# Attention's steps queued per engine, and one weight tile converted per unit instead of two

## The chip, the cores and the metric

One core of a Trainium2 chip. The metric is the device time of one execution in microseconds (us); the kernel before takes 925.54 us, the median of 3 runs (923.69 to 925.55).

Engines are named as in the profile: PE is TensorE's matmul and PEld its weight load, DVE is VectorE, ACT is ScalarE, POOL is GpSimd, SP is SyncE, which issues most transfers.

## The reference

Windowed attention, then two expert layers without routing, one after the other:

```python
# attention: B 4, H 8, S 576, D 64; window 128, one slope per head
scores = where(mask, q @ k.T / sqrt(D) + bias, -1e9)
attn = softmax(scores)                       # over the keys
x = (attn @ v).transpose(0, 2, 1, 3).reshape(2304, 512)
# first layer, d_ff 2048
h = x @ w_in
g = (a0 + a1*h + a2*h*h + a3*h*h*h) / (1 + |b0|*|h| + |b1|*h*h + 1e-6)
x = g @ w_out
# second layer: the same shapes, with elu(h) in place of g
```

The weights of both layers are 64-bit floats in memory, so each tile of them is converted on the chip.

## The kernel before

**Attention.** 16 units of work, each one batch and one pair of heads (`units`). The steps of a unit have short names:
- `qT`, `kT`, `zT`: PE transposes of q, of k and of their last 64 rows (L438, L452); `qC`, `kC`, `zC`: copies of these from PSUM (ACT, DVE, DVE).
- `S0` to `S4`: the scores (PE, L494, L476); `D0` to `D8`: bias and row maximum (DVE, L520, one input in PSUM); `E0` to `E8`: the exponential with its sum (ACT, L535); `R0`, `R1`: the inverse sums (DVE); `N0` to `N8`: the normalising (POOL, L552).
- `T00` to `T11`: 16 transposes of the probabilities (PE, L568); `C00` to `C11`: their copies from PSUM (ACT, L461); `V0`, `V1`, `Y`: the products with v (PE, L587, L598); `XC`, `XY`: their copies into `xT` (ACT, DVE).

`STEPS` is one list for all engines: in each turn `t` of the loop every step is issued once, for unit `t + late`. Each engine keeps that order in its own queue.

**Conversion.** One of the first layer's 32 weight tiles (16 of `w_in`, "wi", and 16 of `w_out`, "wo") takes five operations on 128x512 words: `s` scale (ACT, L130), `a` shift (DVE, L138), `b` or (DVE, L148), `h` the rounded high part (DVE, L156, or ACT, L158), `l` the low part, high part subtracted (DVE, L162). `PLAN` puts two tiles into each of turns 5 to 14. Six further steps of `conv_step` (`CONV_AFTER`) follow in the last turns, and the rest in the first layer, one `conv_step` at every second chunk (`f % 2`). A tile passes `conv_step` in three calls: scale, then shift and or with the next call, high and low part after that.

**First layer.** 5 blocks of tokens (`BL`; block 0 is the first 512 tokens, from batch 0 alone), each with 16 chunks of d_ff. For a chunk `s`, `gemm1(s)` is 12 matmuls into a PSUM bank (`w_in`: high and low parts of weight and token, three products), `rational(s)` is the polynomial quotient, spread over ACT and DVE with the last operation `low` of the chunk before (L339) on POOL from `c > 4` on, and `gemm2_T(s - 3)` is 12 matmuls into the accumulators. The first four chunks of `gemm1` are computed at the end of the attention (`early`, `AHEAD`), and so are `rational(0)` and the first half of `rational(1)` (`FIRST`). Blocks 1 and 2 convert the second layer's weights beside the quotient (`joins`, `load_half`).

**Second layer.** A block scheme with fewer products (`second`), planned by costs written in the code; the change doesn't touch it.

The tiles of weights as loaded (512 KB each) come by SP's queue, two a turn from turn 2 to 13; so do q, k and v (per unit two transfers of 128 KB and one of 32 KB for the last rows of each).

Of the kernel before, what the change touches and what calls it, by code (L numbers as in the profile page):

```python
# [17 lines left out]
STEPS = (  # L18
# [10 lines left out]
)  # L29


PLAN = (0,) * 5 + (2,) * 10 + (0,) * 4
CONV_AFTER = ((15, "E8"), (15, "R1"), (14, "V1"), (15, "T01"), (15, "T11"), (15, "V1"))
AHEAD = {
    (14, "T00"): 1, (14, "T10"): 1, (14, "T11"): 2, (14, "V0"): 1, (14, "V1"): 2, (14, "Y"): 1,
}
ENG = {
    "h0": "D", "h1": "D", "l0": "D", "l1": "D", "qC": "A", "kC": "D",
    "zC": "D", "XC": "A", "XY": "D", "C00": "A", "C01": "A", "C10": "A", "C11": "A",
}  # L40
FIRST = {"r0": (14, "Y"), "r1": (15, "C11")}


@with_exitstack
def kernel(
# [13 lines left out]
    nc = tc.nc  # L59
# [34 lines left out]
    order = [(w, f) for f in range(KF) for w in ("wi", "wo")]  # L94
# [80 lines left out]
    def conv_step(keys, more=True, later=False, eng="A"):  # L175
# [128 lines left out]
    def rational(c, old=True, beside=4 * (lambda: None,)):  # L304
# [38 lines left out]


    def attention():
        with ExitStack() as es:
# [4 lines left out]
            vt = [raw.tile([P, NF + 1, 2, D], F32, name=f"v{n}") for n in range(2)]  # L351
            for t in vt:
                nc.gpsimd.memset(t[TL:P, NF], 0.0)
            units = [(b, p) for p in range(NP) for b in range(B)]
# [4 lines left out]
            qk_tails = place(LATE[3], [P, 3, 2, 2, D], F32, "qk_tails")  # L359

            def load(u, what):
# [3 lines left out]
                for nm in what:  # L365

                    eng = nc.scalar if u < 2 and nm == "k" else nc.sync
                    src = {"q": q, "k": k, "v": v}[nm]
                    if nm == "v":
                        t = raw_t[nm, u] = vt[u % 2]  # L370
                        body, tail = t[:, 0:NF], t[0:TL, NF]
                    else:
                        n = "qk".index(nm)
                        body, tail = raw_t[nm, u] = rows_qk[:, n], qk_tails[0:TL, u % 3, n]
                    for e in range(2):
# [4 lines left out]
                    eng.dma_start(  # L380
                        out=tail,
                        in_=src[b, 2 * p:2 * p + 2, NF * P:S, :].rearrange("h p d -> p h d"),
                    )


# [63 lines left out]
            def qk_tail_T(u):  # L449
                for n, nm in enumerate("qk"):  # L450
                    _, r = raw_t.pop((nm, u))
                    nc.tensor.transpose(  # L452
                        ty[:, n, :], r.rearrange("p e d -> p (e d)"), ident[0:TL, 0:TL]
                    )

            def qk_tail_copy(u):
                copy(ENG["zC"], qkT_t[u][:, :, NF * P:S], ty[:, 0:2, :])
# [119 lines left out]
            def attn_v(i0):  # L577
                def run(u):
                    vr = raw_t["v", u]
                    if i0 == 0:  # L580
# [13 lines left out]
            def attn_v_tail(u):  # L594
                vr = raw_t.pop(("v", u))
                for j in (NF - 1, NF):
                    for e in range(2):
                        nc.tensor.matmul(  # L598
                            ty[e * D:(e + 1) * D, 2, :], lhsT=vr[:, j, e, :],
# [4 lines left out]
            def x_copy(u):  # L604
                b, p = units[u]
                copy("D" if u > NU - 4 else ENG["XC"], xT[:, p, b * S:b * S + NF * P], x_t.pop(u).rearrange("p i c -> p (i c)"))

            def x_tail_copy(eng):
# [733 lines left out]
```

## Time and profile before

| stretch of the span, us | what runs | PE busy | DVE busy | ACT busy | POOL busy |
|---|---|---|---|---|---|
| 0 to 157.0 | attention, 26 tiles scaled, early chunks | 93% | 88% | 90% | 54% |
| 157.0 to 245 | first layer, block 0 | 100% | 93% | 84% | 23% |
| 245 to 400 | first layer, blocks 1 and 2 | 100% | 94% | 84% | 27% |
| 400 to 922.4 | the rest of it, second layer | 99% | 80% | 70% | 7% |

The profiled execution took 924.2 us; its span, from the first to the last instruction, is 922.4 us, and 1.8 us lie around it. TensorE's granted clock is 1.000, the 2.4 GHz level, all the way. A busy share is an average; what limits a stretch is read from the waits in it and from what follows at once on what.

### The profile page before, as it was taken

To read this page: it belongs to the slowest core of one execution; us is meant where nothing else is said; L and a number is where in the kernel's file an instruction comes from. 1 tells how busy PE (TensorE), PEld (TensorE's weight loads), DVE (VectorE), ACT (ScalarE), POOL (GpSimd) and SP (SyncE) were. 2 spreads that over 40 slices of the span, in tenths; PEclk is the share of its full clock that TensorE was granted. 3 is DMA by queue.
4 is the path that set the end of the run, shared out by engine and by line. 5 is a ranking of instruction groups with operands and counts; after the bars stand their busy time and mean duration, and the time that the engine had idled before them with its cause. 6 is when DMAs were issued, how large, how long until landed. Compare 5 with 4: busy or idle time off the path is not lost.

```text
span 922.4 us, 15561 instructions
## 1 busy us (share of the span) xinstructions
PE 907.6 (98%) x5110; PEld 772.2 (84%) x5110; DVE 786.0 (85%) x1761; ACT 710.3 (77%) x1514; POOL 184.5 (20%) x246
## 2 busy tenths in 40 slices
PE   8999998999999999999999999999999999999998
PEld 5777766888888888889988888989888898988887
DVE  7699999999899989978998979999877788677653
ACT  6999997888888888879887877667786667767553
POOL 4566661123222322232322210000000000000000
PEclk9999999999999999999999999999999999999999
DMA  8899971001344244400000124445253323342201
GB/s 157 207 244 217 258 218 53 1 1 34 103 138 138 72 134 130 144 25 1 7 29 0 58 92 128 147 149 194 80 181 101 118 81 111 130 149 84 78 0 69
DMA packets 112561, 98.28 MB, mean 107 GB/s; under 512 B 62816, under 2 KB 86368, under 8 KB 112480
## 3 DMA queue, kind: packets, MB, share of 16 engines
q1 hardware_dynamic: 109936, 96.57, 36.0%
q10 hardware_dynamic: 2544, 0.72, 0.4%
q8 instruction: 40, 0.66, 0.3%
q14 instruction: 41, 0.34, 0.1%
HBM read 79.96 MB, written 17.30 MB: 105 GB/s over the span
## 4 chain that ended last, share of the span: by engine, by line
PE 84%; DVE 11%; ACT 3%; issue 1%; DMA 0%; POOL 0%; ACTq 0%; DVEq 0%; POOLq 0%
PE acc L956 21%; PE acc L730 21%; PE h L289 20%; PE m L940 19%; DVE cvt L148 1%; DVE pr_wi L520 1%; DVE pr_wo L520 1%; PE s_ps L494 1%; PE ps_pT L568 1%; DVE w_wi L162 1%; ACT pr_wo L535 1%; PE x L587 1%; ACT pT L461 1%; DMA qk_tails_wo<-in_k_dram 0%; PE ps_qk L438 0%
## 5 line engine op out<-in xcount | busy, mean ns | idle before, releaser
L730 PE MATMUL acc<-space_g,w_wo 128*128 128x512 f32 (+1 forms) x960 | 210.7, 368 | 2.7 <-DVE space_g L339 2.3
L730 PEld LDWEIGHTS acc<-space_g,w_wo 128*128 128x128 f32 x960 | 168.2, 189 | 33.3 <-DVE space_g L339 2.8
L339 POOL TENSOR_TENSOR space_g<-xT,space_r 128x512 fp32r<-128x512 f32 (+1 forms) x76 | 89.7, 1180 | 295.1 <-DVE xT L338 200.1
L956 PE MATMUL acc<-op_wo,space_g 128*128 128x512 f32 x432 | 108.2, 393 | 0.0
L956 PEld LDWEIGHTS acc<-op_wo,space_g 128*128 128x128 f32 x432 | 80.4, 188 | 14.7
L289 PE MATMUL h<-space_qa,w_wi 128*128 128x512 f32 (+1 forms) x320 | 91.7, 370 | 0.4 <-DVE space_qa L266 0.4
L1002 ACT ACTIVATE space_u<-space_r 128x384 f32<-128x384 f32 x48 | 25.1, 522 | 75.3 <-DVE space_r L996 74.4
L313 ACT ACTIVATE space_u<-h 128x512 f32<-128x512 f32 (+1 forms) x80 | 44.3, 554 | 46.9 <-PE h L289 29.0
L940 PE MATMUL m<-xo_wi,op_wi 128*128 128x384 f32 x336 | 77.3, 337 | 0.0
L940 PE MATMUL m<-xo_wo,op_wi 128*128 128x384 f32 x336 | 76.4, 335 | 0.0
L289 PE MATMUL h<-space_qb,w_wi 128*128 128x512 f32 (+1 forms) x240 | 75.5, 369 | 0.1
L289 PE MATMUL h<-space_ta,w_wi 128*128 128x512 f32 (+1 forms) x240 | 75.4, 368 | 0.0
L325 DVE SCALAR_TENSOR_TENSOR xT<-space_u,b_abs,qa 128x512 f32<-128x512 f32 (+1 forms) x76 | 52.2, 687 | 20.1 <-ACT qa L314 19.9
L289 PEld LDWEIGHTS h<-space_qa,w_wi 128*128 128x128 f32 x320 | 57.7, 189 | 10.8 <-DVE space_qa L266 0.6
L940 PEld LDWEIGHTS m<-xo_wo,op_wi 128*128 128x128 f32 x336 | 60.9, 188 | 4.1
L940 PEld LDWEIGHTS m<-xo_wi,op_wi 128*128 128x128 f32 x336 | 60.5, 188 | 0.0
L322 DVE TENSOR_TENSOR space_g<-xT,space_r 128x512 fp32r<-128x512 f32 (+1 forms) x80 | 55.0, 687 | 5.3
L328 ACT ACTIVATE space_r<-xT,c_q 128x512 f32<-128x512 f32 (+1 forms) x80 | 55.3, 691 | 5.5 <-DVE xT L325 5.3
L315 ACT ACTIVATE xT<-h,a_sb 128x512 f32<-128x512 f32 (+1 forms) x80 | 59.2, 740 | 0.0
L289 PE MATMUL h<-space_bi,w_wi 128*128 128x512 f32 (+1 forms) x160 | 59.0, 369 | 0.2 <-POOL space_bi L269 0.2
L1006 ACT ACTIVATE space_u<-space_u,c_m 128x384 f32<-128x384 f32 x96 | 57.5, 611 | 1.6
L316 ACT ACTIVATE h<-h,a_sb 128x512 f32<-128x512 f32 (+1 forms) x80 | 57.3, 716 | 0.0
(189 smaller groups left out, 2121.8 us busy)
## 6 DMA issues: line engine op xcount, KB each, us to landing
space_qa<-joined_wo SPq DMA_DIRECT2D x43, 256.0 KB, 2.7
raw_wo<-in_moe_w_out_dram SPq DMA_DIRECT2D x20, 512.0 KB, 5.1
raw_wi<-in_moe_w_in_dram SPq DMA_DIRECT2D x16, 512.0 KB, 4.6
half<-in_moe_w_in_dram SPq DMA_DIRECT2D x32, 256.0 KB, 2.8
two_wo<-joined_wi SPq DMA_DIRECT2D x32, 256.0 KB, 2.9
s<-sums SPq DMA_DIRECT2D x32, 256.0 KB, 2.8
half<-in_moe_w_out_dram SPq DMA_DIRECT2D x22, 256.0 KB, 2.9
v<-in_v_dram SPq DMA_DIRECT2D x32, 128.0 KB, 3.6
```

Of the source, the lines that this page charges most:

```text
L289: nc.tensor.matmul(h, lhsT=WT["wi", f][:, SEL[wp], kk * P:(kk + 1) * P], rhs=x[xp][kk], start=(kk == 0 and n == 0), stop=(kk == KD - 1 and ...
L313: nc.scalar.activation(out=h2, in_=h, func=AF.Square)
L315: nc.scalar.activation(out=ee, in_=h, func=AF.Identity, scale=a_sb[:, 1:2], bias=a_sb[:, 0:1])
L316: nc.scalar.activation(out=h, in_=h, func=AF.Identity, scale=a_sb[:, 3:4], bias=a_sb[:, 2:3])
L322: nc.vector.tensor_tensor(out=hi, in0=ee0, in1=rr0, op=ALU.mult)
L325: nc.vector.scalar_tensor_tensor(out=qq, in0=h2, scalar=b_abs[:, 1:2], in1=qa, op0=ALU.mult, op1=ALU.add)
L328: nc.scalar.activation(out=rr, in_=qq, func=AF.Ln, bias=c_q)
L339: (nc.gpsimd if c > 4 else nc.vector).tensor_tensor(out=low, in0=ee0, in1=rr0, op=ALU.mult)
L730: nc.tensor.matmul(acc_t[d], lhsT=WT["wo", f][:, SEL[wp], d * P:(d + 1) * P], rhs=gt[SEL[xp]], start=(f == 0 and n == 0), stop=(f == KF - ...
L940: nc.tensor.matmul(out, lhsT=w[:, SEL[wp], c0:c0 + P], rhs=XO[q // NP2, nm, k][:, SEL[xp]], start=(k == 0 and n == 0), stop=(k == 1 and n ...
L956: nc.tensor.matmul(acc_t[T, t], lhsT=gt[SEL[xp]][:, t * P:(t + 1) * P], rhs=w[:, SEL[wp]], start=(first and n == 0), stop=(last and n == 2),)
L1006: nc.scalar.activation(out=e, in_=e, func=AF.Identity, bias=c_m)
```

## The change

- **Order.** `STEPS`, `PLAN`, `CONV_AFTER`, `AHEAD` and `FIRST` go. `QUEUES` has one list per engine with the lateness of each step, `NEEDS` what must have been issued before a step; the loop at the end of `attention` issues from the four lists whatever is ready, so each engine has its own order.
- **Units** run batch by batch: the four head pairs of batch 0 first. Block 0 needs no later batch. The 16 quarters of the early `gemm1` (`g0` to `g15`), the split of block 0's tokens (`xh`, `xA`, `xl`), the quotient of chunks 0 and 1 (`r0`, `r1`) and the second half of chunk 0's (`o0` to `o3`) become steps of the lists.
- **Conversion.** One tile each for units 1 to 15 (`s0`, `a0`, `b0`, `h0`, `l0`), its low part on POOL (`l0`); the other 17 in block 0: two calls of `conv_step` in chunks 2 to 5, one in chunks 6 to 16, their low part on POOL as well, and ahead of shift and or. `order` puts `wo` three places back.
- **Copies.** 22 of the 64 copies of transposed probabilities and 4 of the 16 of `XC` go to DVE (`ON_DVE`; before, 3 of `XC`). `R0` and `R1` become one `R`.
- **`rational`** gives `low` to POOL from `c > 2` on.
- **Loads.** The last rows of q, k and v come for two units at a time; one weight tile per unit is loaded from unit 0 on, four after unit 14's products with v, the last 13 after unit 15's. The second layer's first halves are loaded at chunk 16 (before, 14), and `joins` skips chunks 17 and 40 in place of 24 and 40.

```diff
+QUEUES = {
+    "PE": (
+        ("g8", 1), ("g2", 2), ("g14", -3), ("g15", -3), ("S4", 3), ("g3", 2), ("g11", -1), ("g12", -2),
+        ("g9", 1), ("Y", 1), ("V1", 1), ("V0", 1), ("kT", 4), ("g4", 2), ("g13", -2), ("T01", 2),
+        ("g5", 2), ("zT", 4), ("T00", 2), ("g0", 3), ("S0", 4), ("S1", 4), ("qT", 5), ("g6", 2),
+        ("T10", 2), ("g1", 3), ("g7", 2), ("T11", 2), ("S2", 4), ("S3", 4), ("g10", 1),
+    ),
+    "ACT": (
+        ("qC", 5), ("XC", 1), ("r0a", 3), ("E3", 4), ("E2", 4), ("E4", 4), ("E8", 4), ("E6", 4),
+        ("E5", 4), ("r1a", 2), ("r1c", -3), ("E7", 4), ("C01", 3), ("xA3", 4), ("xA1", 5), ("C00", 3),
+        ("E0", 4), ("r0c", 3), ("s0", 4), ("E1", 5), ("C10", 3), ("C11", 3),
+    ),
+    "DVE": (
+        ("r1d", -3), ("xh0", 4), ("xl0", 3), ("r0b", 2), ("D5", 3), ("D7", 3), ("b0", 2), ("kC", 4),
+        ("zC", 4), ("D0", 3), ("F01", 2), ("XY", 1), ("o3", -3), ("F00", 2), ("xl1", 3), ("xh2", 3),
+        ("o2", -1), ("r1b", -2), ("D1", 4), ("D3", 4), ("xl2", 3), ("o1", 0), ("R", 3), ("D2", 4),
+        ("o0", 1), ("D4", 4), ("F10", 2), ("xl3", 3), ("r0d", 2), ("F11", 2), ("h0", 2), ("a0", 3),
+        ("D8", 4), ("XD", 1), ("D6", 4),
+    ),
+    "POOL": (
+        ("N0", 2), ("N5", 2), ("N7", 2), ("N1", 2), ("N3", 2), ("N2", 2), ("N6", 2), ("N4", 2),
+        ("N8", 2), ("l0", 1),
+    ),
 }
...
-    order = [(w, f) for f in range(KF) for w in ("wi", "wo")]
+    order = sorted([(w, f) for f in range(KF) for w in ("wi", "wo")], key=lambda k: k[1] + 3 * (k[0] == "wo"))
...
+        if whole:
+            put_off.append(lambda: conv_lo(whole))
         if scaled:
             put_off.append(lambda: conv_shift(scaled))
             put_off.append(lambda: conv_or(scaled))
-        if whole:
-            put_off.append(lambda: conv_lo(whole, "D"))
...
-            (nc.gpsimd if c > 4 else nc.vector).tensor_tensor(out=low, in0=ee0, in1=rr0, op=ALU.mult)
+            (nc.gpsimd if c > 2 else nc.vector).tensor_tensor(out=low, in0=ee0, in1=rr0, op=ALU.mult)
...
-            units = [(b, p) for p in range(NP) for b in range(B)]
+            units = [(b, p) for b in range(B) for p in range(NP)]
...
+            def loads(step, u):
+                if step in ("qT", "kT", "zT") and {(n, u) for n in ("qT", "kT", "zT")} <= gone:
+                    if u + 3 < NU:
+                        load(u + 3, "qk")
+                    if u < NU - 1:
+                        load_some(1)
...
+                elif step in ("V0", "V1", "Y") and {(n, u) for n in ("V0", "V1", "Y")} <= gone:
+                    if u + 2 < NU:
+                        load(u + 2, "v")
+                    else:
+                        load_some(4 if u < NU - 1 else len(to_load))
...
+            while any(queues.values()):
+                for engine, queue in queues.items():
+                    if queue and ready(*queue[0]):
+                        step, u = queue.pop(0)
+                        gone.add((step, u))
...
-            if s >= NCH or f in (0, 8, KF - 1) or s < KF or width(s) < WB or s >= LAST + 3:
+            if s >= NCH or f in (0, KF - 1) or s in (KF + 1, 2 * KF + 8) or s < KF or width(s) < WB or s >= LAST + 3:
...
-            if j == 0 and f % 2:
+            for _ in range(0 if s < 2 or s > KF else 2 if s < 6 else 1):
                 conv_step(to_conv, later=True)
...
-            if s == KF - 2:
+            if s == KF:
                 for n in range(3):
                     load_half(n)
```

## Rows read from the trace of the kernel before

**Rows 1.** The page: busy us, share of the span and instructions of each engine.

```profile
PE 907.6 (98%) x5110; PEld 772.2 (84%) x5110; DVE 786.0 (85%) x1761; ACT 710.3 (77%) x1514; POOL 184.5 (20%) x246
```

**Rows 2.** Busy time by stretch; first line: columns; units without and with two conversions.

```profile
core 0: us, PE busy (x) PEld busy (x) DVE busy (x) ACT busy (x) POOL busy (x), PEclk, DMA share, GB/s
0.00:156.98 156.98, 146.57 (x1369) 108.42 (x1369) 138.15 (x538) 141.23 (x428) 84.25 (x162) 1.00 0.81 199
...
28.28:35.91 7.63, 7.63 (x83) 6.06 (x82) 4.64 (x26) 7.37 (x25) 3.88 (x9) 1.00 0.77 187
76.62:85.06 8.44, 8.22 (x84) 6.08 (x83) 8.37 (x34) 8.33 (x27) 5.57 (x9) 1.00 0.95 212
...
156.98:245.00 88.02, 88.02 (x388) 72.90 (x389) 82.09 (x132) 73.81 (x123) 19.94 (x15) 1.00 0.07 23
```

**Rows 3.** Timeline of PE, units 2 to 4: start, us, engine, line, operation, count.

```profile
20.64 0.54 PE L476 MATMUL s_ps<-space_qa 64*64 64x192 f32 x4
...
28.28 0.54 PE L476 MATMUL s_ps<-space_qb 64*64 64x192 f32 x4
...
29.92 0.88 PE L587 MATMUL x<-pT,v 128*64 128x128 f32 x12
30.73 0.66 PE L438 MATMUL ps_qk<-ident,qk_wi 128*128 128x128 f32 x4
31.32 1.09 PE L587 MATMUL x<-pT,v 128*64 128x128 f32 x16
...
32.57 0.55 PE L568 MATMUL ps_pT<-ident,pr_wi 128*128 128x128 f32 x3
...
33.60 0.93 PE L494 MATMUL s_ps<-space_qa 64*128 64x128 f32 x8
34.45 0.66 PE L568 MATMUL ps_pT<-ident,pr_wo 128*128 128x128 f32 x4
...
35.91 0.54 PE L476 MATMUL s_ps<-space_qa 64*64 64x192 f32 x4
```

**Rows 4.** Timeline of PE, last unit's scores to the first layer.

```profile
126.06 0.54 PE L476 MATMUL s_ps<-space_qb 64*64 64x192 f32 x4
...
145.86 1.63 PE L587 MATMUL x<-pT,v 128*64 128x128 f32 x25 [1.12 <-ACT pT L461]
...
156.98 2.57 PE L730 MATMUL acc<-space_g,w_wo 128*128 128x512 f32 x10 [2.34 <-DVE space_g L339]
```

**Rows 5.** ACT's groups, 0 to 156: count, busy us, mean ns, idle before.

```profile
L461 ACT ACTIVATE pT<-ps_pT 128x512 f32<-128x512 f32 x64 | 34.8, 593 | 0.7 <-PE ps_pT L568 0.6
...
L130 ACT ACTIVATE cvt<-raw_wi 128x512 f32<-128x512 f32 x14 | 9.7, 694 | 1.9 <-DVE w_wo L162 1.0
```

**Rows 6.** DVE's groups, 0 to 156: a copy of 128x512 from PSUM.

```profile
L463 DVE COPY space_qb<-ps_qk 128x512 f32<-128x512 f32 x8 | 5.5, 687 | 0.0
```

**Rows 7.** Timeline of DVE, two chunks of block 0, one with a conversion.

```profile
197.65 0.69 DVE L322 TENSOR_TENSOR space_g<-xT,space_r 128x512 fp32r<-128x512 f32 x1
...
201.57 0.51 DVE L138 TENSOR_SCALAR raw_wi<-raw_wi 128x512 int32<-128x512 int32 x1
...
203.50 0.69 DVE L148 SCALAR_TENSOR_TENSOR cvt<-cvt,raw_wi 128x512 int32<-128x512 int32 x1
...
204.70 0.68 DVE L162 TENSOR_TENSOR w_wo<-cvt,w_wo 128x512 fp32r<-128x512 f32 x1
...
207.45 0.69 DVE L322 TENSOR_TENSOR space_g<-xT,space_r 128x512 fp32r<-128x512 f32 x1
```

**Rows 8.** Timeline of POOL, then of DVE, where block 1's tokens are split.

```profile
222.66 1.36 POOL L269 TENSOR_TENSOR space_bi<-xT,space_qb 128x512 fp32r<-128x512 f32 x1 [1.22 <-ACT space_qb L268]
223.98 1.74 POOL L269 TENSOR_TENSOR space_bi<-xT,space_ta 128x512 fp32r<-128x512 f32 x1
...
222.78 1.78 DVE L162 TENSOR_TENSOR w_wo<-cvt,w_wo 128x512 fp32r<-128x512 f32 x1
224.49 1.78 DVE L322 TENSOR_TENSOR space_g<-xT,space_r 128x512 fp32r<-128x512 f32 x1
```

More of the change, by code (lines that the diff above doesn't have):

```diff
@@ L44 @@
+for n in range(1, 16):
+    NEEDS[f"g{n}"] = NEEDS.get(f"g{n}", ()) + (f"g{n - 1}",)
+for n in "01":
+    NEEDS[f"r{n}b"] = (f"r{n}a",)
+    NEEDS[f"r{n}d"] = (f"r{n}a", f"r{n}b")
 @with_exitstack
@@ new lines, in attention, with runs @@
+                    RUN[f"C{e}{half}"] = probs_T_copy(e, half, "A")
+                    RUN[f"F{e}{half}"] = probs_T_copy(e, half, "D")
+            CONV = {"s0": conv_scale, "a0": conv_shift, "b0": conv_or, "h0": lambda key: conv_hi(key, "D"), "l0": conv_lo}
+            gone = set()
+            end = {}
+            def runs(step, u):
+                if step[0] in "xgro":
+                    return u == NU - 1
+                if step in CONV:
+                    return u > 0
+                if step in ("XC", "XD") or step[0] in "CF":
+                    copies = ON_DVE["XC" if step[0] == "X" else "C" + step[1:]]
+                    return (u in copies) == (step == "XD" or step[0] == "F")
+                return True
@@ new lines, in attention, with end_step @@
+            x1[0] = {}
+            ahead = early()
+            def end_step(step):
+                c = int(step[2]) if step[0] == "x" else int(step[1])
+                if step[0] == "x":
+                    x1[0] = x1[0] or {"hi": [None] * KD, "lo": [None] * KD}
+                    src = xT[:, c, 0:BL[0][1]]
+                    part = "lo" if step[1] == "l" else "hi"
+                    tag = ROW1[f"{part}{c}"][0]
+                    if tag not in end:
+                        end[tag] = cut(tag, SIZE[tag], F32R)
+                    x1[0][part][c] = t = row1(f"{part}{c}", 0)
+                    if step[1] == "l":
+                        nc.vector.tensor_tensor(out=t, in0=src, in1=x1[0]["hi"][c].bitcast(F32), op=ALU.subtract)
+                    elif step[1] == "h":
+                        nc.vector.tensor_copy(t, src)
+                    else:
+                        nc.scalar.activation(out=t, in_=src, func=AF.Copy)
+                elif step[0] == "g":
+                    next(ahead)
+                elif step[0] == "r":
+                    if step[2] == "a":
+                        end.update(first_rational(c))
+                    end[step]()
+                else:
+                    if step == "o0":
+                        es.close()
+                        space_of_chunks()
+                        end.update(first_g())
+                    end[step]()
@@ L713, in attention @@
-            run_all(ahead)
-    def experts():
+            queues = {}
+            for engine, steps in QUEUES.items():
+                lates = [late for _, late in steps]
+                queues[engine] = [
+                    (step, t + late) for t in range(-max(lates), NU - min(lates)) for step, late in steps
+                    if 0 <= t + late < NU and runs(step, t + late)
+                ]
+            needs, held = {}, {"s": [], "p": [], "qk": []}
+            for step, u in queues["PE"]:
+                needs[step, u] = wait = []
+                if step in ("S0", "S2", "S4"):
+                    readers = {"S0": ((1, 3), (2, 4)), "S2": ((5, 7), (6, 8)), "S4": ((0,),)}[step]
+                    for r in readers:
+                        held["s"].append([(f"D{n}", u) for n in r])
+                        if len(held["s"]) > 3:
+                            wait += held["s"][-4]
+                elif step[0] == "T" or step in ("qT", "kT"):
+                    kind, n = ("p", 2) if step[0] == "T" else ("qk", 1)
+                    copies = ("C" + step[1:], "F" + step[1:]) if kind == "p" else (step[0] + "C",)
+                    held[kind].append([(c, u) for c in copies])
+                    if len(held[kind]) > n:
+                        wait += held[kind][-n - 1]
@@ new lines, in ready @@
+            def ready(step, u):
+                wait = needs.get((step, u), []) + [
+                    (n[0], u + n[1]) if isinstance(n, tuple) else (n, u) for n in NEEDS.get(step, ())
+                ]
+                return all(x in gone or not 0 <= x[1] < NU or not runs(*x) for x in wait)
+            while any(queues.values()):
[3 more added lines that the diff above has]
+                        gone.add((step, u))
+                        if step[0] in "xgro":
+                            end_step(step)
+                        elif step in CONV:
+                            key = order[u - 1]
+                            if step == "s0":
+                                to_conv.remove(key)
+                            CONV[step](key)
+                        else:
+                            RUN[step](u)
+                        loads(step, u)
+                        if (step, u) == ("kT", 0):
+                            warm(1)
+                        if (step, u) == ("E4", 2):
+                            nc.scalar.activation(out=b_abs, in_=b_raw, func=AF.Abs)
@@ L719, in experts @@
         cut("w1", WB // 2)
+    def experts():
         def gemm2_T(c):
```

188 lines of the change are left out of this document (98 added, 90 removed), and 15 rows, old and new, of tables (NEEDS, STEPS).

## The prediction, written before the changed kernel was run

> **What bounds the kernel now.** I read the busy shares first, then the stretches, then the timeline of PE where the stretches leave a question. PE is busy 98% of the span [rows 1], so time can be won only where PE waits or where its records are stretched. From 156.98 to 245 PE has 388 matmuls in 88.02 us without a gap [rows 2]: 0.227 us each, 2.72 us for 12, 5.44 us for a chunk (`gemm1` and `gemm2_T`). PE sets that stretch, and the two layers behind it, which the change leaves nearly as they are. What is open is the attention, 0 to 156.98, and whether block 0 stays bound by PE.
>
> In the attention there are two regimes. A unit without conversion takes 7.63 us: PE never stops, ACT is at 7.37 and DVE at 4.64 us. A unit with two conversions takes 8.44 us: DVE 8.37 and ACT 8.33, PE's real work the same 83 matmuls [rows 2]. So conversions push the unit from PE's limit to DVE's and ACT's. From the last unit's scores at 126.06 to the first layer's second product at 156.98 stands the drain, with PE waits of 1.12 us for ACT and 2.34 us for DVE, among others [rows 4].
>
> **The change, part by part.**
>
> *PE's own order.* The lists hold the same PE work. Eight transposes take 1.03 us (32.57 to 33.60), twelve take 1.46 (34.45 to 35.91) [rows 3]: 0.108 each and 0.16 for the change of tile shape. Per unit I count eight groups of one tile shape in `STEPS` and eight in `QUEUES`: `V0`, `V1` and `Y` become one group, `zT` becomes one by itself. PE's unit stays 7.64 us; one group more or less is 0.16.
>
> *Loads of a unit on the other engines.* ACT: 7.37, less 22/16 copies and 1/16 of `XC` at 0.59 less 0.09 overlap (back-to-back records overlap by about 0.09), plus one scale at 0.69 less 0.09 [rows 2, 5]: 7.37 - 0.72 + 0.60 = 7.25. DVE: two conversions cost it 8.37 - 4.64 = 3.73, one 1.87; without the low part (0.68 less 0.08 [rows 7]) 1.27; 23/16 copies more at 0.60 [rows 6] 0.86; one `R` fewer I leave out: 6.77. POOL: 3.88 in a unit without conversion [rows 2], plus a low part at 1.36 [rows 8]: 5.24, with up to 1.7 of waiting as in the units with two conversions (5.57). All lie under 7.64, so PE sets every unit. From the scores of unit 2 at 20.64, 13 units give 20.64 + 13 x 7.64 = 119.9 for unit 15, now 126.06 [rows 3, 4]: **-6.2 us**. Ends: 8.0 a unit (the in-order queues leave half of the excess) gives 124.6, -1.4; 7.5 a unit gives -8.
>
> *The drain.* From 126.06 PE has left: 48 matmuls of the early `gemm1`, 10.9; two units' transposes of probabilities, 32 x 0.108 and six changes, 4.4; three sets of `V0`, `V1`, `Y` (0.81 from 29.92 to 30.73 and 1.25 from 31.32 to 32.57 [rows 3]), 6.2; `S2`, `S3` 1.2; two matmuls of chunk 0's second product, 0.5: 23.2 us of work in 30.9 us. Batch-first units make the early quarters free of the last units, and five of them stand behind the last `Y` on PE (3.4 us) while DVE does `o0` to `o3`. I take the whole difference, **-7.7**; if PE goes on waiting for half of it, -4. What waits newly: `r0a` on ACT stands behind `g3`, with the copies of the last unit behind it; `o0` on DVE waits for the last `V1` and `Y` (its space is theirs), with `o1` to `o3`, `r1b`, `r1d` behind it, some 4.9 us of DVE for 3.4 us of PE. That second wait can cost 1 to 2 us and is in the -4.
>
> *Seventeen conversions in block 0 in place of six.* Here DVE is the engine to add up. Two chunks with one conversion take it 197.65 to 207.45, 9.80 us; the conversion in it is shift 0.43, or 0.60, low part 0.60 [rows 7], so a plain chunk is 4.08. With its low part on POOL a conversion leaves 1.03 on DVE: 5.11 for a chunk with one, 6.14 for one with two, against PE's 5.44. That would be nearly free, if POOL's part were. It isn't: while POOL subtracts 512 columns, a DVE operation with two inputs in SBUF takes 1.78 in place of 0.68, and it happens twice, at 222.78 and 224.49, once for each of POOL's two [rows 8]. So a low part on POOL stops DVE for up to 1.1 us, unless DVE is then at an operation that reads PSUM (L325, L341, L342, 0.6 to 0.7 each). L341 and L342 already cover POOL's `low`. In a chunk with one conversion L325 covers about 0.6, which leaves 0.5: 5.6 against 5.44, 11 chunks (6 to 16), +1.9. In chunks 3 to 5 two low parts cost 0.5 + 1.1: 7.75 each. Chunk 2 takes 6.2 from a start at PE's first second product, so chunk 5's quotient, on which `gemm2_T(4)` waits, ends at 6.2 + 3 x 7.75 = 29.4; PE would like it at 4 x 5.44 + 0.45 = 22.2: +7.2. Together **+9.1**. Ends: +2.4 when POOL's parts stop nothing (6.2 + 3 x 6.14 = 24.6 against 22.2, and no loss after), +17.4 when nothing covers them (below).
>
> The Trainium skill ("SBUF — State Buffer", Who interferes with whom) calls this an exclusive lock: a DVE operation with two SBUF inputs and a GpSimd operation that reads SBUF don't share, one blocks fully. The two records of 1.78 agree. By it moving the low parts to GpSimd is a transfer of DVE's time into DVE's waiting, not a saving; with full blocking and no cover the sum is the third rival's.
>
> *With one answer each.* ACT in block 0: 4.1 a plain chunk by 73.81 us of 16, six conversions included [rows 2], plus scale and high part, 0.6 each: 5.3 with one, under 5.44; 6.5 with two, under DVE's 7.75. The order of tiles (`wo` three back): chunk 9 needs tile 16 and has 15 done plus ten, no wait. The last 13 tiles are loaded after unit 15's products; the first of them is converted in chunk 4, over 10 us later; free while that lead holds, and the DMA engines at 0.81 of the stretch [rows 2] get fewer bytes in it, not more. Half the loads of last rows: fewer issues on SP, for which nobody waits. Halves at chunk 16 and `joins` from 18: one chunk of 5.44 us covers them. POOL's `low` from chunk 3: counted above.
>
> **The sum.** 922.4 - 6.2 - 7.7 + 9.1 = 917.6 of span, with 1.8 around it 919.4, against the profiled 924.2. The median of the runs is 1.3 above that execution, so I forecast **920.5**.
>
> **Rivals.**
> 1. *POOL's low parts stop nothing* (they fall beside L341, L342, L325 or wait themselves). For it: DVE's operations don't lengthen in any chunk of block 0 where POOL has only `low`. Against: rows 8, and two operations of 1.3 a chunk for 2 us of cover. 922.4 - 13.9 + 2.4 = 910.9, 914.0 as a median.
> 2. *The units don't get under 8.0* (each engine at over 85% in order; a step late on ACT stands before the copies that PE needs). For it: ACT's list has `C01` in the middle, waiting for PE's next turn. Against: units at 7.63 with ACT at 7.37 show that 97% can be had [rows 2]. 922.4 - 1.4 - 7.7 + 9.1 = 922.4, 925.5: no change.
> 3. *Slower: the lock without cover.* Place: block 0, DVE. Price: 1.1 for each of 17 low parts. Chunks 3 to 5 take 8.3 (end 31.1, +9.0), chunks 6 to 16 take 6.2, 0.76 over PE's, +8.4: +17.4, and 922.4 - 13.9 + 17.4 = 925.9, 929.0. It decides from where block 0 loses more than the 13.9 that the attention gains, that is from 0.85 per low part on.
>
> **How the numbers follow.** Forecast 0.45 (its own range 916 to 925, from the drain's -4 and +-0.3 of lock a chunk), rival 1 0.25, rival 2 0.15, rival 3 0.15. The range leaves out the outer part of rivals 1 and 3: **911 to 929**. A measurement of this kernel tells 0.2% (1.9 us) from no change. Faster: most of the forecast, rival 1 and little of rival 2, 0.66. Same: the upper end of the forecast and most of rival 2, 0.15. Slower: rival 3 and rival 2's upper end, 0.19.
>
> **What the new profile would show.** Scores of unit 15 near 121 and a spacing of 7.6 between units (8.0 or more: rival 2). The first product of the accumulators on PE near 143 (over 147: the drain isn't won). In the 30 us after it, PE waits of 7 us for POOL's `low` or DVE, and DVE operations of block 0 with two SBUF inputs at 1.2 to 1.8 us: the lock; none: rival 1; waits that go on to chunk 16 at 0.7 each: rival 3. From block 1 on the two profiles should run in parallel; a difference there would be something that I haven't seen, and so would a PE wait for a weight tile.

## The result, and the profile of the changed kernel

The changed kernel ("after") takes **935.36 us** (935.10 to 935.73, 4 runs) against 925.54: ratio **1.0111**, interval 1.0094 to 1.0129. I had forecast 920.5 and a range to 929. It is slower, outside the range, on the other side. The profiled execution took 935.59, its span 933.8, against 924.2 and 922.4 before.

The busy line of after, beside [rows 1]: PE has 5 us more (matmuls at half clock, below), POOL 40 us more, DVE and ACT a little less. Shares don't show where 11 us went.

```profile
PE 912.6 (98%) x5110; PEld 774.7 (83%) x5110; DVE 785.1 (84%) x1709; ACT 706.3 (76%) x1500; POOL 225.0 (24%) x279
```

The stretches do (beside [rows 2]; the third and fourth are two units of the attention, the fifth runs from the first second product to the split of block 1's tokens, the last holds that split).

```profile
core 0: us, PE busy (x) PEld busy (x) DVE busy (x) ACT busy (x) POOL busy (x), PEclk, DMA share, GB/s
0.00:146.06 146.06, 141.06 (x1366) 106.63 (x1367) 119.59 (x471) 122.16 (x389) 99.95 (x176) 1.00 0.77 180
30.03:38.28 8.25, 7.86 (x85) 5.99 (x83) 7.15 (x28) 6.82 (x24) 5.92 (x11) 1.00 1.10 212
53.63:61.35 7.72, 7.72 (x84) 5.99 (x83) 6.36 (x27) 6.92 (x24) 5.95 (x12) 1.00 0.62 152
146.06:233.06 87.00, 75.65 (x303) 58.89 (x301) 78.66 (x114) 70.17 (x116) 34.77 (x27) 0.94 0.16 57
233.06:247.06 14.00, 13.58 (x47) 10.54 (x48) 13.63 (x17) 9.82 (x17) 8.64 (x6) 0.78 0.18 57
```

The attention is PE's now: a unit of 7.72 us has 7.72 us of PE. In the 87 us behind it PE, busy without a gap before, does 303 of some 384 matmuls, and its mean granted clock is 0.94. The timeline of PE names the places (scores of units 1, 2, 14, 15, then the records of block 0 with a wait, without three of some 0.3 us in chunks 10 to 12; beside [rows 3, 4]).

```profile
16.66 0.54 PE L560 MATMUL s_ps<-space_qb 64*64 64x192 f32 x4
22.39 0.54 PE L560 MATMUL s_ps<-space_qa 64*64 64x192 f32 x4
...
116.23 0.54 PE L560 MATMUL s_ps<-space_qa 64*64 64x192 f32 x4
123.44 0.54 PE L560 MATMUL s_ps<-space_qb 64*64 64x192 f32 x4
...
146.86 2.58 PE L876 MATMUL acc<-space_g,w_wo 128*128 128x512 f32 x10 [0.19 <-DVE space_g L427]
161.22 3.90 PE L876 MATMUL acc<-space_g,w_wo 128*128 128x512 f32 x10 [3.17 <-POOL space_g L383]
169.81 2.57 PE L876 MATMUL acc<-space_g,w_wo 128*128 128x512 f32 x10 [1.49 <-POOL space_g L383]
178.39 4.64 PE L876 MATMUL acc<-space_g,w_wo 128*128 128x512 f32 x10 [2.84 <-POOL space_g L383]
...
232.03 0.93 PE L333 MATMUL h<-space_qa,w_wi 128*128 128x512 f32 x2 [2.61 <-ACT space_qa L312]
233.45 0.80 PE L333 MATMUL h<-space_qb,w_wi 128*128 128x512 f32 x1 [0.49 <-DVE space_qb L313]
```

Ten products that took 2.57 take 3.90 and 4.64 after a wait. The granted clock stands at 0.5 (1.2 in place of 2.4 GHz) for 3.4, 6.8 and 6.8 us, each time beginning within 0.7 us of the end of such a wait:

```profile
160.00:165.00 5.00, 3.78 (x11) 3.02 (x12) 3.59 (x5) 2.26 (x5) 3.71 (x3) 0.66 0.00 2
165.00:177.00 12.00, 9.06 (x39) 6.83 (x37) 9.39 (x16) 9.27 (x16) 4.16 (x4) 1.00 0.01 2
177.00:185.00 8.00, 6.61 (x16) 5.21 (x17) 7.66 (x11) 7.04 (x13) 4.42 (x4) 0.57 0.00 0
232.00:240.00 8.00, 7.45 (x18) 5.01 (x19) 7.97 (x10) 5.83 (x10) 5.65 (x4) 0.57 0.10 31
```

One number per place carries the rest of this text: the **lead**, the start on PE of chunk c's first second product, minus the same of before (162.11, 183.87, 221.94 and 232.82 us for chunks 1, 5, 12 and 14); negative is earlier. After: -10.1 at chunk 1, +2.5 at chunk 5, +4.0 at chunk 12, **+11.4** from chunk 14 to the end of the kernel. So the attention won 10.1, block 0 lost 21.5, and nothing happens behind it: 922.4 - 10.1 + 21.5 = 933.8, the span.

Who is late in block 0 is read from DVE and POOL, one chunk (beside [rows 7, 8]; L366, L369, L382, L385, L386 are L322, L325, L338, L341, L342 of before, L383 is POOL's `low`, L206 the conversion's low part).

```profile
207.34 1.29 POOL L383 TENSOR_TENSOR space_g<-xT,space_r 128x512 fp32r<-128x512 f32 x1 [3.52 <-DVE xT L382]
208.59 1.28 POOL L206 TENSOR_TENSOR w_wi<-cvt,w_wi 128x512 fp32r<-128x512 f32 x1
...
207.81 0.69 DVE L386 TENSOR_TENSOR xT<-xT,h 128x512 f32<-128x512 f32 x1
208.63 1.79 DVE L366 TENSOR_TENSOR space_g<-xT,space_r 128x512 fp32r<-128x512 f32 x1
210.35 0.73 DVE L369 SCALAR_TENSOR_TENSOR xT<-space_u,b_abs,qa 128x512 f32<-128x512 f32 x1
211.00 0.42 DVE L182 TENSOR_SCALAR raw_wo<-raw_wo 128x512 int32<-128x512 int32 x1
...
214.68 1.79 DVE L366 TENSOR_TENSOR space_g<-xT,space_r 128x512 fp32r<-128x512 f32 x1
```

A chunk of DVE takes 214.68 - 208.63 = 6.05 us against PE's 5.44, and 1.1 of it is L366 at 1.79 in place of 0.69. POOL's L206 begins at 208.59, when L383 ends, 0.04 ahead of L366, and L366 ends once L206 is through. L386 (one input in PSUM) runs at 0.69 beside L383. The same comes in nine chunks in a row (178.38 to 226.80). The three chunks with two calls ahead of them take DVE 7.3, 8.7 and 8.6.

### The profile page after: what moved, and what is told of

Read it like the earlier page. It is cut to its first block, busy times and chain, and to the rows that moved or that the text cites. A ratio compares the mean times of both kernels' runs of the same rounds, so it can differ in the third digit from the quotient of the medians.

```text
span 933.8 us, 15528 instructions
## 1 busy us (share of the span) xinstructions
PE 912.6 (98%) x5110; PEld 774.7 (83%) x5110; DVE 785.1 (84%) x1709; ACT 706.3 (76%) x1500; POOL 225.0 (24%) x279
## 4 chain that ended last, share of the span: by engine, by line
PE 85%; DVE 11%; issue 2%; ACT 1%; POOL 1%; DVEq 0%; POOLq 0%; ACTq 0%
PE acc L1102 21%; PE m L1086 18%; PE acc L876 17%; PE h L333 17%; PE ps_pT L652 3%; PE s_ps L578 3%; PE x L671 3%; PE ps_qk L522 2%; DVE space_g L366 2%; DVE cvt L192 1%; DVE xT L369 1%; DVE xT L386 1%; DVE h L385 1%; DVE xT L382 1%; PE s_ps L560 1%
## 5 line engine op out<-in xcount | busy, mean ns | idle before, releaser
L876 PE MATMUL acc<-space_g,w_wo 128*128 128x512 f32 (+1 forms) x960 | 216.5, 374 | 8.6 <-POOL space_g L383 8.4
L876 PEld LDWEIGHTS acc<-space_g,w_wo 128*128 128x128 f32 x960 | 170.5, 192 | 42.4 <-POOL space_g L383 11.3
L383 POOL TENSOR_TENSOR space_g<-xT,space_r 128x512 fp32r<-128x512 f32 (+1 forms) x78 | 92.0, 1180 | 267.2 <-DVE xT L382 212.1
L369 DVE SCALAR_TENSOR_TENSOR xT<-space_u,b_abs,qa 128x512 f32<-128x512 f32 (+1 forms) x76 | 52.1, 685 | 21.7 <-ACT qa L358 21.6
L366 DVE TENSOR_TENSOR space_g<-xT,space_r 128x512 fp32r<-128x512 f32 (+1 forms) x79 | 65.1, 824 | 5.7
```

The costliest lines, as they stand in the source:

```text
L366: nc.vector.tensor_tensor(out=hi, in0=ee0, in1=rr0, op=ALU.mult)
L369: nc.vector.scalar_tensor_tensor(out=qq, in0=h2, scalar=b_abs[:, 1:2], in1=qa, op0=ALU.mult, op1=ALU.add)
L383: (nc.gpsimd if c > 2 else nc.vector).tensor_tensor(out=low, in0=ee0, in1=rr0, op=ALU.mult)
L876: nc.tensor.matmul(acc_t[d], lhsT=WT["wo", f][:, SEL[wp], d * P:(d + 1) * P], rhs=gt[SEL[xp]], start=(f == 0 and n == 0), stop=(f == KF - ...
```

## The experiments

Leads and times of all kernels (each time is a median of fast runs, compared with runs of before made on the same chip); the diffs below show what each kernel changes:

| kernel | lead at 1 | at 5 | at 12 | at 14 | us | ratio |
|---|---|---|---|---|---|---|
| after | -10.1 | +2.5 | +4.0 | +11.4 | 935.4 | 1.0111 |
| lo_dve | -10.1 | -0.3 | -0.3 | +6.4 | 929.5 | 1.0034 |
| lo_zero | -10.1 | -1.2 | -1.2 | -1.2 | 924.5 | 0.9978 |
| no_words | -10.1 | -9.1 | -9.1 | -9.1 | 915.1 | 0.9879 |
| warm | -10.1 | -0.3 | +4.0 | +10.3 | 934.9 | 1.0096 |
| late_zero | -10.1 | -6.3 | -6.3 | -6.0 | 918.2 | 0.9921 |
| late | -10.1 | +0.8 | +5.1 | +9.9 | 934.2 | 1.0096 |
| late_dve_d | -10.1 | +8.6 | +23.3 | +33.8 | 957.4 | 1.0346 |
| gap | -10.1 | +5.2 | +5.2 | +10.2 | 934.5 | 1.0090 |
| x5 | -6.6 | -2.9 | +15.6 | +24.8 | 948.8 | 1.0251 |
| x5_gap | -6.6 | -6.0 | -5.3 | +1.3 | 925.5 | 1.0000 |
| x5_pair | -6.6 | -6.1 | -5.0 | +1.9 | 925.2 | 0.9997 |
| x3_pair | -7.6 | -7.0 | +2.3 | +2.3 | 927.3 | 1.0019 |
| after_lolast | -10.1 | +1.0 | +4.0 | +9.3 | 933.6 | 1.0099 |
| x5_lolast | -6.6 | -6.0 | -5.4 | 0.0 | 924.8 | 0.9999 |
| x3_lolast | -7.6 | -7.0 | -0.6 | -0.6 | 928.8 | 1.0044 |
| x5_soon | -6.5 | -2.6 | -2.4 | -1.4 | 923.1 | 0.9977 |
| x5_soon1 | -6.6 | -4.0 | -3.4 | -0.9 | 923.5 | 0.9980 |

(x3_lolast falls to +4.3 at chunk 16.)

**What the conversions in block 0 cost, piece by piece.**

```diff
 # lo_dve
-            put_off.append(lambda: conv_lo(whole))
+            put_off.append(lambda: conv_lo(whole, "D"))
 # lo_zero
+            put_off.append(lambda: zero_lo(whole))   # nc.gpsimd.memset(..., 0.0)
 # no_words: lo_zero, and
-            put_off.append(lambda: conv_shift(scaled))
-            put_off.append(lambda: conv_or(scaled))
 # warm: 3, 1 and 3 products of zeros between the second products of chunks 2, 3, 4
```

> The changed kernel with one difference: in block 0 the low part of a converted tile is subtracted on DVE (0.60 us of its time) in place of POOL. Lock theory (each of the 17 subtractions on POOL holds a DVE operation for 1.1 us): DVE gets shorter chunks although it has more to do, 5.7 in place of 6.06 us with one conversion and 7.3 in place of 8.5 with two; 922 to 926 us, and DVE's L366 back at 0.69 us. Amount theory (block 0 simply has more conversion work than DVE can take): 17 x 0.60 = 10 us more on DVE, 935 to 945 us. Clock theory (the stretches at half clock cost it): as many waits, so still three such stretches and 935 us.

> The changed kernel, but for the 17 tiles of block 0 POOL writes zeros in place of the low part (the subtraction is left out; a write that reads nothing). DVE and ACT have the same operations. Lock theory: DVE's records fall back to 0.69 us, a chunk with one conversion is 5.1, with two 6.1; only some 2.4 us are lost in block 0 against PE's pace, 917 to 920 us. Amount theory: DVE's and ACT's work is the same, so 933 to 935 us.

> As lo_zero, and shift and or of the 17 tiles are left out as well, so that DVE has nothing to do for the conversions of block 0 (ACT still scales and rounds them). This is the price of the attention alone: the first layer at PE's pace from 146.9 us on, 915 us by both theories. Lock theory: within 3 us of lo_zero. Amount theory: some 18 us under lo_zero.

> The changed kernel with matmuls of a zero weight into an accumulator where PE waits for POOL's low of chunks 2, 3 and 4 (3, 1 and 3 of them, 0.93 us each at full clock), so that PE isn't idle there. Clock theory (the two stretches at half clock between 160 and 173 us of the span cost 6 us of the loss): those stretches vanish, 929 us. Lock theory (DVE sets the pace of block 0, and a faster PE only waits more): the clock stays at 1.0 there, but the waits of chunks 5 to 9 come back, 933 to 936 us.

`no_words`, which leaves out shift, or and low part, gave its 915: of the attention's -10.1, -9.1 are left, so block 0 still loses 1.0 with ACT's scales and high parts and POOL's zeros. It stands 9.4 us under `lo_zero`, more than the lock theory's 3 and less than the amount theory's 18. `lo_zero` took 12.6 off after's lead, so POOL's subtractions cost that much. Eight of its chunks in a row take 4.95 us where after's take 6.06. In its timelines of POOL and DVE, POOL writes in the same place, and L370 (L366 of after) keeps its 0.69.

```profile
217.04 0.53 POOL L214 MEMSET w_wo<- 128x512 f32 x1
...
217.09 0.69 DVE L370 TENSOR_TENSOR space_g<-xT,space_r 128x512 fp32r<-128x512 f32 x1
```

But it missed 917 to 920 by 5 us, and its chunks with two calls still took 7.3, 8.3 and 8.1: a second price. `lo_dve` wins back 5.0 of after's 21.5 us, as doing the subtraction on DVE (0.6) is dearer than nothing and cheaper than being stopped by it (1.1): chunks of 5.41 with L366 at 0.68, no loss from chunk 5 to 12; it missed 922 to 926, with chunks of 9.3, 8.4 and 8.25 at the two calls and 6.7 us lost at the split.

```profile
211.32 0.68 DVE L366 TENSOR_TENSOR space_g<-xT,space_r 128x512 fp32r<-128x512 f32 x1
...
216.73 0.68 DVE L366 TENSOR_TENSOR space_g<-xT,space_r 128x512 fp32r<-128x512 f32 x1
```

`warm` kept the clock at 1.00 in chunks 2 to 4, and DVE's chunks stayed the same (7.2, 8.7, 8.6, 6.7, 6.06): PE only waits in other places. The half clock in those chunks is a consequence.

```profile
177.00:185.00 8.00, 7.49 (x29) 5.10 (x28) 7.66 (x11) 7.02 (x13) 4.42 (x4) 1.00 0.00 0
```

**The second price: a ring of two engines.** The waits of lo_zero from 146 to 180 (engine, tile, line, what it waited for: us in total, times, longest):

```profile
ACT w_wi L202 <- DVE cvt L192: 6.7, 3, 2.3
...
DVE xT L373 <- ACT qa L362: 3.4, 2, 1.7
DVE xT L373 <- ACT xT L362: 2.6, 2, 1.7
```

In a chunk with two conversions the second call puts its high part on ACT ahead of the chunk's Square and Abs. That high part waits 2.3 us for DVE's or (L192), the Abs behind it is late, and DVE's L373 waits 1.7 us for the Abs.

```diff
 # late_zero (from lo_zero) and late (from after)
-            for _ in range(0 if s < 2 or s > KF else 2 if s < 6 else 1):
-                conv_step(to_conv, later=True)
...
+                def calls():        # behind the chunk's first four ACT operations
+                    for _ in range(0 if s < 2 or s > KF else 2 if s < 6 else 1):
+                        conv_step(to_conv, later=True)
+                    go_on()
+                rational(s, beside=(calls, lambda: None, go_on, go_on))
 # late_dve_d: late, low parts on DVE, split_x(1, lows="DDDD")
```

> lo_zero (POOL writes zeros for block 0's low parts, which are left out of the computation) with one thing moved: block 0's conversion calls stand behind the chunk's first four ACT operations instead of ahead of them. The amount of DVE's and ACT's work is the same. Ring theory: in lo_zero's chunks 2 to 5 ACT's second high part waits some 2.3 us for DVE's or with the next Square and Abs queued behind, and DVE's L369 then waits 1.7 us for ACT; with the calls moved these waits go, chunks 3 to 5 fall from 8.2 us to 6.1 to 6.5, and the time from 924.5 to 917 to 920. Amount theory: chunks with two conversions are 8.2 us because DVE and POOL have that much to do; the time stays within 2 us of 924.5.

> The kernel after with the same move of the calls alone, POOL's subtractions kept. If the ring and the lock are two separate prices, this gains what late_zero gains over lo_zero: 928 to 931 by the ring theory, and chunks 6 to 14 stay at 6.0 us. If DVE's extended instructions already fill chunks 3 to 5 under the lock, nothing is gained: 934 to 936, chunks 3 to 5 at 8.6 us.

> The kernel after with the calls moved, block 0's low parts on DVE, and all four low parts of the split for block 1 on DVE. From lo_dve's 929.5: the ring's share (some 4 us, if late_zero shows it) goes, and the lock at the split, where lo_dve lost 5 us (from -0.3 at c=12 to +5.1 at c=13), goes in part: estimate 922 to 925. If the split's 5 us are an amount of DVE work and not the lock, it stays at 925 to 928.

`late_zero` is the ring theory's: chunks 3 and 4 of 6.5 and 6.4 us, 918.2, 4.7 us of lead. Neither of the two waits above is left between 146 and 180; the longest of ACT for DVE there is 1.6 us. `late` gains only 1.45, as its second theory said: its chunks are 8.2 and 8.1 us, and in the later ones the stop has moved from L366 to L382.

```profile
210.55 1.70 POOL L206 TENSOR_TENSOR w_wi<-cvt,w_wi 128x512 fp32r<-128x512 f32 x1 [2.36 <-ACT w_wi L202]
...
211.00 1.79 DVE L382 TENSOR_TENSOR xT<-xT 128x512 f32<-128x512 f32 x1
```

So the two prices don't add: 4.7 without the subtractions, 1.45 with them. `late_dve_d` is a plain miss, 32 us over its estimate: DVE's low part now waits up to 2.4 us for a high part that ACT makes in the same chunk ("DVE w_wo L206 <- ACT w_wo L202: 22.5, 10, 2.4"), and DVE's chunks take 10.3 to 11.9 us at the two calls and 7.86 behind them. The place that opens one ring closes another, because the low part changed its engine.

**What stops and what doesn't.**

```diff
 # gap: in chunks 2 to 16
 ACT  Square, Abs, ...        -> Abs, Square, ...
 DVE  L366, L369, shift, L377 -> L369, shift, L366, L377
 # x5, x5_gap: five tiles more in the attention, one call a chunk in block 0
+EXTRA = (3, 6, 9, 11, 13)    # units; x5 from late_dve_d, x5_gap from gap
```

> The kernel after with DVE's order in block 0's chunks 2 to 16 changed: L369 of the new chunk and the shift stand ahead of L366 of the old one, and on ACT Abs ahead of Square; nothing is added or taken away. In the traces of after, L385, L386 and L369, each with one input in a PSUM bank, ran at 0.68, 0.69 and 0.74 us beside POOL's subtractions, and L366, L377, L192, L382, with both inputs in SBUF, at 0.68 or 1.8. Theory of the lock by operands: with 2.5 us of such instructions in a row (0.68 + 0.69 + 0.74 + 0.42), POOL's L383 and the low part, 2.57 us back to back, meet none of the others: L366 falls from 1.80 to 0.7 us, chunks 6 to 14 from 6.06 to 5.0 to 5.4 us, and the time from 935.4 to 928 to 931 (chunks 2 to 5 and the split keep their price). Theory that whatever DVE does loses 1.1 us per low part: the 1.1 us turns up in another instruction, chunks stay at 6.0 us and the time at 934 to 937.

> late_dve_d with five more tiles converted in the attention (units 3, 6, 9, 11, 13) and one call in each chunk of block 0. The attention's units are set by PE at 7.7 us; DVE, ACT and POOL have room there for one more tile in five units if the lock does not lengthen DVE past PE: then the first second-product stays at 146 to 148, block 0's chunks 3 to 5 fall to 5.4 us, and the time to 914 to 919. If the units with two tiles become DVE's (8.5 us and more), each costs 1 us or more: 919 to 925.

> gap with five more tiles converted in the attention (units 3, 6, 9, 11, 13), so that block 0 has one call in each chunk, at the place where after has it, and no ring. x5 showed the price of the five tiles in the attention: its second products stood 6.64 us ahead of before at chunk 1, where after's stood 10.1 ahead. If the lock goes by operands, chunks 3 to 14 run at PE's 5.44 us and the lead of 6.6 us is kept to the split, which takes 0.4 to 5 us of it: 919 to 924, under both kernels. If the low part takes its 1.1 us wherever it stands, chunks are 6.0 us, 7 us go from chunk 3 on and the split takes 5 to 7 more: 930 to 933.

`gap` is the theory of the operands': beside POOL's L206 now stand L376 and the shift (L369 and L182 of after), and L366 is back at 0.68. The shift isn't left alone: it reads one tile of SBUF and takes 0.62 here, where in after, with POOL idle, it took 0.42 (above).

```profile
209.90 1.29 POOL L206 TENSOR_TENSOR w_wi<-cvt,w_wi 128x512 fp32r<-128x512 f32 x1
...
210.19 0.75 DVE L376 SCALAR_TENSOR_TENSOR xT<-space_u,b_abs,qa 128x512 f32<-128x512 f32 x1 [0.39 <-ACT space_u L361]
210.85 0.62 DVE L182 TENSOR_SCALAR raw_wo<-raw_wo 128x512 int32<-128x512 int32 x1
211.39 0.68 DVE L366 TENSOR_TENSOR space_g<-xT,space_r 128x512 fp32r<-128x512 f32 x1
```

Chunks take 5.5 us and nothing is lost from chunk 5 to 12. The time missed 928 to 931: in the chunks with two calls L376, now first in DVE's chunk, waits up to 2.3 us for ACT ("DVE xT L376 <- ACT space_u L361: 8.4, 4, 2.3"), which loses 2.7 us more than in after, and the split takes 5.0. `x5` has late_dve_d's ring and its loss, and missed both its ranges by 23 us and more. `x5_gap` has one call a chunk: 0.6 us lost from chunk 1 to 5 where after lost 12.6, at the price of 3.5 us of the attention. It missed its 919 to 924 by the split, 6.6 us. In the kernels that take gap's order the shift can meet POOL's subtraction; in x5_soon (L184) it takes 1.07 once and ends only 0.3 us behind one:

```profile
208.81 1.30 POOL L208 TENSOR_TENSOR w_wo<-cvt,w_wo 128x512 fp32r<-128x512 f32 x1
209.33 1.07 DVE L184 TENSOR_SCALAR raw_wo<-raw_wo 128x512 int32<-128x512 int32 x1
```

**The split of block 1's tokens**, where after loses 7.4 of its 21.5 us. PE of x5_gap, then of x5_soon from 145 to 260 (its last record with a wait):

```profile
220.31 0.73 PE L335 MATMUL h<-space_qa,w_wi 128*128 128x512 f32 x2 [0.71 <-ACT space_qa L314]
223.09 0.79 PE L335 MATMUL h<-space_qb,w_wi 128*128 128x512 f32 x1 [2.05 <-DVE space_qb L315]
```

```profile
158.23 3.44 PE L905 MATMUL acc<-space_g,w_wo 128*128 128x512 f32 x10 [1.93 <-DVE space_g L398]
```

```diff
 # x5_pair, x3_pair: gemm1(15) issued with gemm1(14); split_x(1, lows="DDDD")
 # *_lolast: in gemm1(16) the products with the inputs' low parts last
+        if c == KF:
+            pairs.sort(key=lambda p: PASS[p[1]][1] == "lo")
 # x5_soon, x5_soon1: x5_lolast, lows="DDDD", calls from chunk 0 (1) in place of 2
 # x3_*: EXTRA = (6, 9, 13)
```

> x5_gap with two more changes at the split of block 1's inputs, where x5_gap lost 6.6 us (lead -5.33 at chunk 12, +1.27 from chunk 14 on; PE waited 0.71 and 2.05 us and then ran 6.8 us at half clock): the first products of chunk 15 stand right behind those of chunk 14, so that PE has two chunks' second products (5.4 us) instead of one's while the split is made, and all four low parts of the split are DVE's, so that POOL locks nothing there. Theory that the 6.6 us are the split's latency on DVE and ACT, doubled by the clock: no PE wait at the split, the lead of 5.3 us is kept but for 0 to 1 us, and the time is 918.5 to 920.5. Theory that DVE has too much work there, wherever PE stands: DVE's 2.8 us for the four low parts come out as PE waits one chunk later, and the time is 922 to 926.

> x5_pair with three of the five extra tiles (units 6, 9, 13), and so fourteen tiles left for block 0, still one call in each chunk. In x5 the five tiles cost 3.5 us of the attention's lead, some 0.7 us a tile. If that is a price per tile, this is 1.4 us faster than x5_pair: 917 to 919. If the price is set by the last units (11 and 13) or block 0 needs its tiles earlier than one call a chunk gives them, it is no faster: 919 to 922.

> The kernel after with one change: in the first group of first products of block 1 (chunk 16) the four products that need the inputs' low parts come last instead of every third. In after PE waits there 2.61 us for ACT's first rounded part, 0.49 us for DVE's first low part and then runs 6.8 us at half clock, 7.4 us in all. If the loss is DVE's work, or ACT's lateness with its 2.61 us, at most 0.5 us goes: 934.5 to 935.5. If it is the second wait that brings the clock down, 0.5 + 3.4 us go: 931 to 932.

> x5_gap with the same change of the order of chunk 16's products. x5_gap waited 0.71 us for ACT, 2.05 us for DVE's first low part and lost 6.6 us between chunks 12 and 14, 3.4 of them by 6.8 us at half clock; the second wait now meets a product that PE reaches some 1.8 us later. Theory that the split's price is the order in which PE meets the parts (latency and the clock behind it): 3 to 5 us of the 6.6 go, 920.5 to 922.5. Theory that it is DVE's amount of work, which x5_pair bore out for another place of the waits: the wait moves to a later chunk, 924.5 to 926.

> x5_lolast with three of the five extra tiles (units 6, 9, 13). In x3_pair the attention's lead at chunk 1 was 7.56 us instead of 6.62, and chunks 3 to 10 kept it as in x5_pair; what it lost came from chunk 15's first weight tile, asked for a chunk early there and not here. So by the first theory of x5_lolast 1 us under it, 919.5 to 921.5; by the second 924 to 925.5; if the weight tile of chunk 15 is late here too, 926 to 930.

> x5_lolast with block 0's calls beginning two chunks earlier (chunk 0 instead of 2), so that the last tile is whole two chunks earlier and DVE and POOL have no conversion beside the split (a shift, an or and a low part, some 1.1 us of DVE and 1.3 of POOL a chunk, less in the two chunks before the split), and with the split's four low parts on DVE. x5_lolast still lost 5.4 us there (PE waits 0.73, 0.52 and 1.18 us and 3.4 us at half clock). Theory that this is the amount of DVE's work and POOL's lock around the split: DVE is 2 us and more ahead when the split comes, the waits fall under 1 us in all and 4 us go: 920 to 922. Theory that it is the order of the two engines at the split, which this leaves as it is (ACT's rounding behind Exp, DVE's low parts behind the chunk's last operation): 923.5 to 925. If the earlier calls delay the first chunks, where DVE still ends the attention, up to 2 us are lost at chunk 1 in either case.

> x5_soon with the calls beginning at chunk 1. By the theory of the amount half of x5_soon's gain at the split (2 us), 922 to 923.5, unless chunk 0's call costs x5_soon its gain at the start; by the theory of the order 923.5 to 925, the same as x5_soon.

`x5_pair` gave PE 2.7 us more between chunk 15 and the split, and the loss stayed (6.9): DVE comes to the split as late as before. `x5_lolast` got 1.2 of 6.6, `after_lolast` 2.2 of 7.4, between its two cases: 0.5 of waiting, and 3.4 us at half clock in place of 6.8, which is 1.7 of time. That second part isn't shown to come from the order: warm, late and gap have 3.4 us at half clock there with the order of after. So the order in which PE meets the parts, and the clock behind, are the smaller share, 1.2 to 2.2 us. `x5_soon` took the conversions away from the two chunks before the split, and the loss there is 0.9; `x5_soon1`, with one chunk less, 2.5. This looks like the theory of the amount, but most of it is not won: DVE begins the split's low parts at 222.97 in x5_soon and at 222.28 in x5_lolast, 0.7 later, and it is PE that comes 3.0 us later (lead -2.4 for -5.4 at chunk 12). At chunk 14 x5_soon stands 1.4 us ahead of x5_lolast, and this is all that the earlier calls and the four low parts on DVE are worth together.

What the loss mainly goes by is how far DVE is behind PE when it begins the low parts, counted from PE's start of chunk 12's second products:

| kernel | DVE behind PE, us | lost at the split, us |
|---|---|---|
| lo_zero, late_zero | 1.1 | 0 to 0.4 |
| x5_soon | 3.4 | 0.9 |
| gap | 4.7 | 5.0 |
| x5_soon1 | 4.9 | 2.5 |
| lo_dve | 5.2 | 6.7 |
| x5_lolast, x5_gap | 5.7 | 5.4 to 6.6 |
| after, after_lolast | 6.7 | 7.4, 5.2 |
| x5 | 8.7 | 9.2 |

A lead that PE has and DVE doesn't is for the most part lost there. (Against gap, x5_soon1 loses half at nearly the same distance, so the order of the products and the engine of the low parts count too; they weren't tried one by one.) The call in chunk 0 costs x5_soon 3.9 us at chunk 2 (1.93 of waiting, the clock at half for 3.4 us behind it), so it ends at **923.1 us, ratio 0.9977** (0.9968 to 0.9986), between its two cases (920 to 922 and 923.5 to 925), 0.2% faster than before. The `x3` kernels lose at a tile: in both PE waits for a tile's high and low part (4.4 and 2.0 us in x3_pair; 1.6 and 2.1, then 1.9 and 1.0 us in x3_lolast), as fourteen tiles at one a chunk come too late (x3_pair's second case, at a higher price than it named, and x3_lolast's third).

## Why the prediction was wrong

**Right: PE sets the units; the drain.** Spacing 7.64 to 7.72 in nine of thirteen units, 7.20 in the last, 8.25 in three, with 0.39 of waiting in the one shown. From the last scores to the second products -7.5 (23.42 from 123.44 to 146.86, 30.92 before [rows 4]; forecast -7.7).

**Mis-sized: the units' -6.2.** Scores of unit 15 came at 123.44, -2.6. Unit 2 began at 22.39 where 20.64 was taken over from before [rows 3] (+1.75), and 13 units at 7.77 in place of 7.64 are +1.7. Together the attention gave -10.1 for a forecast -13.9. Three slips of the working change nothing: 20.64 + 13 x 7.64 is 119.96, so that term is -6.1; 919.4 + 1.3 is 920.7; and the unit with two conversions has 84 matmuls in [rows 2], not 83.

**Failed: block 0's +9.1, measured +21.5.** Three steps of it:

1. *"In a chunk with one conversion L325 covers about 0.6, which leaves 0.5: 5.6 against 5.44"*. It covers nothing. POOL's low part doesn't fall on L325; it begins when POOL's `low` ends, which is when DVE starts L322, and the measured chunk is 6.06, the whole 1.1. The third rival had that mechanism and 6.2 a chunk, and I gave it 0.15; its 929.0 was still 6.4 us short, for the two steps below. lo_zero prices the subtractions at 12.6 us over the whole of block 0. What I should have done is lay POOL's two operations along DVE's order: 2.57 us of POOL, and behind L341 and L342 (1.4 us) stands L322. gap shows that the cover can be had, by order, not by hope.
2. *"6.5 with two, under DVE's 7.75"* for ACT. Sums of busy time can't see a ring: neither engine was full, both waited for each other in turn. Price 4.7 us where the subtractions don't hide it (late_zero), 1.45 where they do (late).
3. *The split*, which has rows of its own among those I read [rows 8], had no term. It loses nothing where DVE has kept near PE (lo_zero, 4.95 a chunk) and 5 to 7.4 us where DVE's chunk is 5.4 or more (lo_dve, gap, x5_gap, after). By the table of the split it goes mainly by how late DVE arrives; which part of DVE's work would have to go to win it isn't shown, as x5_soon changes two things and wins 1.4.

One order of adding the 21.5: 1.0 for scales and high parts (no_words), 3.1 for shift and or at their best place (late_zero), 4.7 for the ring (lo_zero), 12.6 for POOL's subtractions, the split's 7.4 among them. In another order the shares differ, as late shows.

The Trainium skill ("SBUF — State Buffer", Who interferes with whom) says that an instruction of VectorE with two SBUF inputs and one of GpSimd that reads SBUF exclude each other, the one that starts first having the ports to its end, and that one with at most one SBUF input, outside VectorE's two-port modes, or a GpSimd instruction that only writes, is left alone. The rows agree: L366 at 1.79 beside the subtraction, 0.69 beside the memset, L376 at 0.75 beside the subtraction. The shift, with one SBUF input, is stopped all the same (1.07 for 0.42), and no run here shows in which mode it runs. The prediction weighed the rule and took half of its price without a row for the cover.

"A PE wait for a weight tile" and "a difference behind block 1" were to show something unseen; neither came in after.

## What to carry to other kernels

Before work goes to an engine whose instructions stop another's, as in [rows 8], write both engines' instructions of one period side by side and see which instruction of the first stands where the second's begin; a cover that no row shows counts as none. Where two in-order queues feed each other twice a period, follow the dependencies round once: a sum of busy times under the period doesn't say that it fits. A stretch where PE has just been made faster needs the margin of its feeders recomputed everywhere, at the rare steps too. And a loss that shrinks at one place is counted at the next place where all kernels agree again, since the engine that waited may only have come later.

## What the runs showed of the hardware

PE's granted clock went to half for 3.4, 6.8 or (late_dve_d) 10.2 us, each time near waits of PE. The length of a wait doesn't tell when: waits of 2.0 (warm), 2.3 (lo_zero) and 2.5 us (lo_dve) left it at 1.00, and in x5_lolast it fell behind 0.73, 0.52 and 1.18 us. Nor does it tell for how long: the same wait in chunk 4 had 6.8 us at half clock in after (2.84 us) and 3.4 in after_lolast (2.85). The half clock cost nothing where DVE set the pace (warm, at chunk 12) and counted where PE had no later wait to absorb it (at x5_gap's split 2.8 of the 6.6 us are waits, and 6.8 us at half clock cost some 3.4, an estimate: half of them).

POOL's next subtraction starts some 0.04 us before its last one ends, and so comes ahead of a DVE instruction that starts at that end: 1.1 us to the loser each time, nine chunks in a row.
